# An attention block on one core: one addition of the early chains moved from VectorE to an accumulating transfer

## The chip, the cores and the metric

The kernel runs on one NeuronCore of a Trainium2 chip. The core has five engines that run side by side, each with its own instruction queue, worked off in order: TensorE (PE) multiplies matrices, VectorE (DVE) and ScalarE (ACT) work element by element, GpSimd (POOL) does simple passes over SBUF and can issue transfers, and SyncE (SP) issues most transfers. Sixteen DMA engines carry out the transfers. The metric is the time on the device in microseconds (us), lower is better.

## The reference

```
qkv = (x @ wqkv).reshape(B, S, 3, H, Dh).transpose(2, 0, 3, 1, 4)
q, k, v = qkv[0], qkv[1], qkv[2]
scores = einsum("bhqd,bhkd->bhqk", q, k) * Dh ** -0.5
p = softmax(scores, axis=-1)
o = einsum("bhqk,bhkd->bhqd", p, v)
out = o.transpose(0, 2, 1, 3).reshape(B, S, D) @ wo
```

B = 1, S = 2048 positions, D = 448 columns, H = 16 heads of Dh = 28; everything is bf16.

## The kernel before

**Sets and steps.** The 16 heads form four groups of four, each head padded to 32 rows, so that a group fills 128 partitions. The 2048 queries form four blocks of 512. A group and a block of queries make a *set*; there are 16, worked off in the order of `ORDER`. A *step* is one head of a set against one block of 128 keys: scores of 128 keys by 512 queries. A set has 4 x 16 = 64 steps. Scores of up to four heads run in TensorE at once, in different row groups; the products of the probabilities with the values (tile `o`, line 987) likewise, a *wave* of four heads in four column groups. A row of ones in the values gives the softmax denominator; there is no pass for the maximum, a bound worked out from the norms of queries and keys goes into the scores as additional rows of `QP`.

**Two ways to exponentiate.** ScalarE takes two steps in one instruction (`do_exp`, line 891: tile `a`, two banks wide, gives `pt`; there are ten `pt` tiles). VectorE takes one step (`do_a`, line 906) from a bank `d0`, `d1` or `m`: it adds a constant to the scaled score, clips at zero and writes int16, whose bits read as bf16 are a straight-line approximation of the exponential. One such line is coarse. So three lines are summed: four steps of a set form a *chain* with one int16 tile `I4` of 128 x 2048; the second and third line are `I4` plus 43 and plus 85 (`SHIFT`, added on VectorE in `do_add`, line 929, tiles `J1` and `J2`), and TensorE multiplies each of the three tiles with its own scaled copy of the values (`VT[k]`). So a step on VectorE costs one line, half an addition of four steps' width, and three value matmuls, where a step on ScalarE has one value matmul.

**The order.** Python code plays the five engines forward with assumed durations when the kernel is built, and emits each instruction when its engine is free: `pick_pe`, `pick_dve`, `pick_pool` and so on. The order of each engine's queue is fixed by this; on the chip, semaphores keep the dependencies. `d_more` opens a chain when fewer than `NCH` = 3 chains are in use and gives VectorE steps whenever a score bank is free; the remaining steps go to ScalarE. `pending` lists the tiles that wait for their value matmuls, each with the time at which it is expected, and `pv_cands` offers those whose time has come. `port` holds the times to which VectorE's additions and GpSimd's passes occupy what the code takes as a shared port: `can_add` in `pick_dve` lets no addition start in the planned time of a GpSimd pass, and `best` the other way round.

**GpSimd's passes** are, in the main part, the squares of keys and queries (line 297, for the norms) and the multiplication of a finished set by its reciprocals (line 1038). The reciprocals take this way (`finish_set`): VectorE copies the output bank `o` to `o_sb` (line 1016), SP gathers the denominators into `den`, VectorE inverts them, SP writes them to DRAM (`scr`) and spreads them over the partitions into `rr` (line 1035, 256 KB), GpSimd multiplies. The bank `o` is there once, so the next set's value matmuls wait for the copy.

**Other work on TensorE** is fitted in through bank `m`: the projections to keys, queries and values of coming groups (gated by the count of steps), norms, and the output projection. Where TensorE would idle for long, multiplications by zero (`dense`) are put in.

## Time and profile before

| what | value |
|---|---|
| median of 3 runs | 369.49 us (368.03 to 369.72) |
| the profiled execution | 368.69 us, span 366.9 us |
| granted TensorE clock | 1.000 |
| VectorE lines `I` | 292, 680 ns each |
| VectorE additions `J` | 146, all 128 x 2048, 724 ns each |
| ScalarE exponentials | 366, 1145 ns each, overlapping |
| GpSimd squares | 27 after the start, 1041 ns median |
| GpSimd multiplications | 15, 1263 to 1787 ns |
| transfers | 12.30 MB, mean 34 GB/s |

The span is the time from the first to the last instruction of one profiled execution. In the groups of instructions a line gives the source line, the engine, the operation, the tile written and the tiles read, the shape and the count; then busy time and mean duration; then the idle time before them and what ended it. Durations of successive instructions overlap on an engine, so an instruction's duration is longer than its share of the engine's time.

### The profile page before, as it was taken

What the parts mean: (1) busy time and instruction counts of PE and PEld (TensorE: products, weight loads), DVE (VectorE), ACT (ScalarE), POOL (GpSimd) and SP (SyncE); (2) the same over time, 40 slices, a digit from 0 to 9 for tenths busy, and PEclk for the clock granted to TensorE, in tenths of its full rate; (3) what the DMA queues carried; (4) which work ended last, traced back from release to release, by engine and by line L of the source; (5) the groups of instructions that cost most, each with busy time, mean ns of one, the idle gap of its engine ahead of it and who ended that gap; (6) DMA issues with size and microseconds to landing.
All of it is one profiled execution on the core that took longest, in us unless ns stands there. A gap on an engine that the chain in (4) does not pass through costs nothing.

```text
span 366.9 us, 10993 instructions
## 1 busy us (share of the span) xinstructions
PE 345.5 (94%) x4528; PEld 112.3 (31%) x4529; DVE 347.6 (95%) x646; ACT 348.9 (95%) x381; POOL 70.8 (19%) x103
## 2 busy tenths in 40 slices
PE   8999999999999999999889999989988999999985
PEld 4433233422233333232222222222222222222223
DVE  7799999999899999899999999999999999999983
ACT  4689999999999999999999999999999999999992
POOL 8952122123010413121010413201010101010010
PEclk9999999999999999999999999999999999999999
DMA  8510100011000000010000001100000001010101
GB/s 256 123 42 15 28 29 7 4 35 36 18 31 28 6 6 30 15 42 28 15 19 3 30 3 55 31 21 12 19 14 9 26 29 54 19 65 27 46 14 50
DMA packets 15050, 12.30 MB, mean 34 GB/s; under 512 B 6808, under 2 KB 13080, under 8 KB 15000
## 3 DMA queue, kind: packets, MB, share of 16 engines
q1 hardware_dynamic: 13448, 10.18, 9.7%
q10 hardware_dynamic: 1040, 1.02, 0.9%
q8 instruction: 35, 0.57, 0.7%
q0 software_dynamic: 512, 0.40, 0.5%
q14 instruction: 15, 0.12, 0.1%
HBM read 7.58 MB, written 1.96 MB: 26 GB/s over the span
## 4 chain that ended last, share of the span: by engine, by line
PE 34%; ACT 30%; DVE 27%; issue 7%; DMA 1%; DVEq 0%; ACTq 0%
ACT pt L891 30%; DVE I L906 12%; PE a L699 12%; PE o L987 9%; DVE J L929 7%; PE m L289 4%; PE m L282 4%; DVE QP L180 1%; DVE V L540 1%; DVE QA L436 1%; DVE KA L315 1%; DVE z L495 1%; PE d L699 1%; DVE o_sb L1016 1%; DVE V L552 1%
## 5 line engine op out<-in xcount | busy, mean ns | idle before, releaser
L891 ACT ACTIVATE pt<-a 128x1024 bf16<-128x1024 f32 x366 | 337.6, 1145 | 3.0 <-PE a L699 1.4
L906 DVE TENSOR_SCALAR I<-d 128x512 int16<-128x512 f32 x263 | 170.7, 680 | 3.8 <-PE d L699 3.4
L699 PE MATMUL a<-QP,KA 32*128 32x512 bf16 (+1 forms) x720 | 141.0, 381 | 12.2 <-ACT pt L891 11.2
L987 PE MATMUL o<-pt,V 128*32 128x512 bf16 x732 | 104.2, 384 | 0.0
L929 DVE TENSOR_SCALAR J<-I 128x2048 int16<-128x2048 int16 x146 | 101.8, 724 | 0.3
L699 PEld LDWEIGHTS <-KA 32*128 32x128 bf16 (+1 forms) x1041 | 48.7, 91 | 151.2 <-issue 148.3
L699 PE MATMUL d<-QP,KA 32*128 32x512 bf16 (+1 forms) x258 | 83.3, 383 | 1.3 <-DVE I L906 1.3
L987 PE MATMUL o<-J,V 128*32 128x512 bf16 x584 | 76.6, 384 | 0.4 <-DVE J L929 0.3
L987 PE MATMUL o<-I,V 128*32 128x512 bf16 x292 | 68.6, 384 | 0.7 <-DVE o_sb L1016 0.5
L987 PEld LDWEIGHTS <-V 128*32 128x32 bf16 x1608 | 28.6, 94 | 49.6 <-issue 47.0
L1038 POOL TENSOR_TENSOR xs<-o_sb,rr 128x512 bf16<-128x512 f32 x12 | 16.4, 1370 | 105.9 <-DMA rr<-scr 65.0
L282 PE MATMUL m<-XT,WRAW 112*32 112x512 bf16 x384 | 29.6, 384 | 0.2 <-DVE V L540 0.2
L297 POOL TENSOR_TENSOR sq<-KA 128x512 bf16<-128x512 bf16 x12 | 12.5, 1041 | 69.6 <-DVE KA L315 69.6
L297 POOL TENSOR_TENSOR sq<-QA 128x512 bf16<-128x512 bf16 x15 | 16.4, 1091 | 47.4 <-DVE QA L436 47.4
L906 DVE TENSOR_SCALAR I<-m 128x512 int16<-128x512 f32 x29 | 19.7, 680 | 0.4 <-PE m L699 0.4
L289 PE MATMUL m<-WRAW,XT 112*32 112x112 bf16 (+1 forms) x768 | 18.1, 230 | 0.2 <-DVE V L540 0.2
L1038 POOL TENSOR_TENSOR OTL<-o_sb,rr 128x512 bf16<-128x512 f32 x3 | 4.2, 1403 | 56.0 <-DMA rr<-scr 36.7
L289 PEld LDWEIGHTS <-XT 112*32 112x32 bf16 x768 | 11.7, 96 | 10.3 <-issue 10.1
L289 PE MATMUL m<-WO,xs 128*32 128x448 bf16 x156 | 12.5, 359 | 0.0
L436 DVE CAST QA<-m 128x512 bf16<-128x512 f32 x15 | 10.2, 683 | 1.1 <-PE m L282 0.5
L699 PE MATMUL m<-QP,KA 32*128 32x512 bf16 x29 | 11.1, 384 | 0.0
L289 PE MATMUL m<-sq,maskK 128*32 128x512 bf16 x108 | 10.8, 388 | 0.1
(113 smaller groups left out, 192.0 us busy)
## 6 DMA issues: line engine op xcount, KB each, us to landing
rr<-scr SPq DMA_DIRECT2D x15, 256.0 KB
QP<-QA SPq DMA_DIRECT2D x60, 28.0 KB
out_dram<-osb SPq DMA_DIRECT2D x12, 112.0 KB
WRAW<-in_wqkv_dram SPq DMA_DIRECT2D x3, 392.0 KB
xs<-in_x_dram ACTq DMA_DIRECT2D x4, 224.0 KB
xs<-in_x_dram SPq DMA_DIRECT2D x4, 224.0 KB
QP<-su SPq DMA_DIRECT2D x32, 2.0 KB
out_dram<-pt SPq DMA_DIRECT2D x2, 224.0 KB
```

Of the source, the lines that this page charges most:

```text
L180: nc.vector.memset(QP[c][k][z][:], 0.0)
L282: nc.tensor.matmul(out=ps[HP * i:HP * (i + 1), :], lhsT=w[:, cc, h * Dh:h * Dh + HP], rhs=XT[c][cc // 2][:, cc % 2, :], start=(cc == 0), s ...
L289: nc.tensor.matmul(out=out[r, :], lhsT=lhsT[:, r], rhs=rhs, start=start, stop=stop, tile_position=(0, HP * i), **k)
L297: nc.gpsimd.tensor_tensor(out=t[:], in0=src, in1=src, op=ALU.mult)
L315: nc.vector.tensor_scalar(out=KAt[(g, sc)][:], in0=src, scalar1=kmask[:, 0:1], scalar2=ones[:, 0:1], op0=ALU.mult, op1=ALU.add)
L436: nc.vector.tensor_copy(out=t[:], in_=held[key][:, 0:QW])
L699: nc.tensor.matmul(out=out_ap, lhsT=KAt[(g, j // XB)][r, (j % XB) * P:(j % XB + 1) * P], rhs=q[r, :], start=(n == 0), stop=(n == len(terms ...
L891: nc.scalar.activation(out=pt[:], in_=ps[:], func=ACT.Exp, scale=LN2 / 128.0)
L906: nc.vector.tensor_scalar(out=dst, in0=pd[:], scalar1=BIAS, scalar2=0.0, op0=ALU.add, op1=ALU.max)
L929: nc.vector.tensor_scalar(out=r[:, w], in0=ch["I"][:, w], scalar1=float(SHIFT[k]), scalar2=None, op0=ALU.add)
L987: nc.tensor.matmul(out=o[HP * i:HP * (i + 1), :], lhsT=VT[e["k"]][g, j // XB][:, j % XB, HP * i:HP * (i + 1)], rhs=e["ap"], start=(SETMM[k ...
L1038: nc.gpsimd.tensor_tensor(out=otile(g, c), in0=st["o_sb"][:], in1=st["rr"][:], op=ALU.mult)
```

## The change

A chain that is opened when its set has at least `FAR` = 24 steps left (the one just taken not counted) is called *far*. For a far chain GpSimd fills the `J1` tile with the constant 43 in every int16 (a memset of 1024 words of 32 bits), and when the four lines are in `I4`, GpSimd issues a transfer that adds `I4` onto `J1` in place. The code expects it to have landed 6.0 us after an issue that takes 0.65 us, and plans the value matmuls of `J1` for then. VectorE makes only the addition for `J2`. For other chains VectorE makes both, as before.

Every GpSimd pass gets a wait for the VectorE operation last emitted among those that use the shared port (`after_shared`; `cur["shared"]` is set by the additions, the scaled values, the norms' small operations and the reciprocals). The transfer's issue does not get it.

Buffers: `I4` and `J1` four instead of three, `J2` three; a chain is opened by new conditions (`dve_ok`) that look at the chain four before. To make room, `osb` has two tiles instead of four, `o_sb` and `rr` one instead of two, and the first query tile shares its buffer with `z`. The copy to `o_sb` needs the multiplication of the set before (`("OT",) + set_gc(s - 1)`). Assumed durations: GpSimd's square 1.08 instead of 1.15, the multiplication 1.3 instead of 1.4, the spread's landing 7.0 instead of 5.5, and the inversion is planned 2.0 later.

```diff
+    NCH = 4
+    NCH2 = 3
+    NJ = 4
+    FAR = 24
+    ACC_LAND = 6.0
...
+        if op.after is not None:
+            op.after(end)
...
+    def after_shared(m):
+        if "shared" in cur:
+            tc.add_manual_dep(m.ins, cur["shared"].ins.name,
+                              mybir.DependencyInfo(mybir.DependencyClass.Sync, mybir.DependencyReason.DATA),
+                              reason="GpSimd's pass stays behind VectorE's")
...
-        nc.gpsimd.tensor_tensor(out=t[:], in0=src, in1=src, op=ALU.mult)
+        after_shared(nc.gpsimd.tensor_tensor(out=t[:], in0=src, in1=src, op=ALU.mult))
...
     def dve_ok(t, k):
-        if chain["cur"] is None and chain["used"] >= NCH:
-            return False
+        if chain["cur"] is None and len(chain["all"]) >= NCH:
+            old = chain["all"][-NCH]
+            if not j1_free() or not used_up(old, 0) or any(a[0] is old for a in adds) or old["acc"] is None or old["acc"] > t:
+                return False
...
+                chain["all"].append(ch)
+                ch[1] = wk.tile([P, HG * QW], I16, name="J1", bufs=NJ)
+                if sum(len(q) for q in remain[step[0]]) >= FAR:
+                    ch["far"] = True
+                    far_chain(ch)
...
+    def close(ch, m):
+        ch["m"] = m
+        adds.append([ch, m, 2 if ch["far"] else 1])
+        if ch["far"]:
+            accumulate(ch, m)
+
+    def used_up(ch, k):
+        return ch["m"] is not None and ch["got"][k] == ch["m"]
+
+    def j1_free():
+        return len(chain["all"]) < NJ or used_up(chain["all"][-NJ], 1)
+
+    def add_ok(a):
+        if a[2] == 1:
+            return True
+        n = chain["all"].index(a[0])
+        return n < NCH2 or used_up(chain["all"][n - NCH2], 2)
+
+    def far_chain(ch):
+        n = len(chain["all"])
+        fill = SHIFT[1] * 65537
+
+        def emit():
+            m = nc.gpsimd.memset(ch[1][:].bitcast(I32), fill)
+            after_shared(m)
+
+        ch["id"] = n
+        add("POOL", 1.08, emit, gives=[("fill", n)], pri=20, port=True)
+
+    def accumulate(ch, m):
+        w = slice(0, m * QW)
+        ch["acc"] = None
+
+        def emit():
+            nc.gpsimd.dma_start(out=ch[1][:, w], in_=ch["I"][:, w], accum_op=ALU.add)
+
+        def landed(end):
+            at = ch["acc"] = end + ACC_LAND
+            for n in range(m):
+                pending.append({"step": ch["steps"][n], "k": 1, "ap": ch[1][:, n * QW:(n + 1) * QW].bitcast(BF16),
+                                "ready": at, "pt": None, "ch": ch})
+
+        evt[("I4", ch["id"])] = (free["DVE"], "DVE")
+        add("POOL", 0.65, emit, need=[("fill", ch["id"]), ("I4", ch["id"])], gives=[("acc", ch["id"])], pri=10, port=True)
+        ops["POOL"][-1].after = landed
...
-        nc.vector.tensor_scalar(out=r[:, w], in0=ch["I"][:, w], scalar1=float(SHIFT[k]), scalar2=None, op0=ALU.add)
+        cur["shared"] = nc.vector.tensor_scalar(out=r[:, w], in0=ch["I"][:, w], scalar1=float(SHIFT[k]), scalar2=None, op0=ALU.add)
...
-            st["o_sb"] = wk.tile([P, QW], F32, name="o_sb")
+            st["o_sb"] = wk.tile([P, QW], F32, name="o_sb", bufs=1)
...
-        add("DVE", 0.61, evac, need=[("Oset", s)], gives=[("osb", s)], rel="o", pri=-5)
+        add("DVE", 0.61, evac, need=[("Oset", s)] + ([("OT",) + set_gc(s - 1)] if s else []), gives=[("osb", s)], rel="o", pri=-5)
...
-        add("DVE", 0.16, recip, need=[("den", s)], gives=[("rec", s)], pri=50, port=True)
+        add("DVE", 0.16, recip, need=[("den", s)], gives=[("rec", s)], pri=50, lag=2.0, port=True)
...
-        add("SP", 0.5, spread, need=[("scr", s)], gives=[("rr", s)], land=5.5, pri=2)
-        add("POOL", 1.4, mul, need=[("rr", s)], gives=[("OT", g, c)], pri=60, port=True)
+        add("SP", 0.5, spread, need=[("scr", s)], gives=[("rr", s)], land=7.0, pri=2)
+        add("POOL", 1.3, mul, need=[("rr", s)], gives=[("OT", g, c)], pri=60, port=True)
...
-        can_add = adds and port["POOL"] <= t
+        can_add = adds and port["POOL"] <= t and add_ok(adds[0])
```

More of the change, by code (lines that the diff above doesn't have):

```diff
@@ L33, in __init__ @@
         self.need, self.gives, self.pri = list(need), list(gives), pri
+        self.after = None
         self.acq, self.rel, self.gate, self.lag, self.land, self.cols, self.port = acq, rel, gate, lag, land, cols, port
@@ L73 @@
     NPT = 10
-    NCH = 3
+    NCH = 4
[3 more added lines that the diff above has]
+    ACC_LAND = 6.0
     DRAIN = 8
@@ L322, in k_job @@
         add("DVE", 0.72, evac, need=[key + (split - 1,)], gives=[key], rel=bank, pri=pri)
-        add("POOL", 1.15, lambda: square(key, KAt[(g, sc)][:]), need=[key], gives=[("ksq", g, sc)], pri=pri, port=True)
+        add("POOL", 1.08, lambda: square(key, KAt[(g, sc)][:]), need=[key], gives=[("ksq", g, sc)], pri=pri, port=True)
     def kn_job(g, bank, pri, gate=0):
@@ L342, in spread_rows @@
             kmt[g] = wk.tile([P, 1], F32, name="kmt")
-            nc.vector.reduce_max(out=kmt[g][:], in_=b[:], axis=AX.X)
+            cur["shared"] = nc.vector.reduce_max(out=kmt[g][:], in_=b[:], axis=AX.X)
         for sc in range(NQC):
@@ L428, in evac @@
             if first:
-                t = qtt[0] = wk.tile([P, QW], BF16, name="qt0", bufs=1)
+                t = qtt[0] = wk.tile([P, QW], BF16, name="z", bufs=1)
             else:
@@ L452, in q_job @@
         else:
-            add("POOL", 1.15, lambda: square(key, QAt[(g, c)][:]), need=[key], gives=[("qsq", g, c)], pri=pri, port=True)
+            add("POOL", 1.08, lambda: square(key, QAt[(g, c)][:]), need=[key], gives=[("qsq", g, c)], pri=pri, port=True)
             add("SP", 2.4, rows, need=[key, ("QZ", c, g % 2)] + ([("Oset", ORDER.index((g - 2, c)))] if g > 1 else []),
@@ L497, in bound @@
             held[("su",) + key] = su = wk.tile([P, QW], BF16, name="su", bufs=1)
-            nc.vector.tensor_scalar(out=su[:].bitcast(I16), in0=z[:].bitcast(I16), scalar1=0.5, scalar2=HALFE,
+            cur["shared"] = nc.vector.tensor_scalar(out=su[:].bitcast(I16), in0=z[:].bitcast(I16), scalar1=0.5, scalar2=HALFE,
                                     op0=ALU.mult, op1=ALU.add)
@@ L551, in scale @@
             flat = (lambda v: v.rearrange("p t g e -> p (t g e)")) if g is None else (lambda v: v.rearrange("p t e -> p (t e)"))
-            nc.vector.tensor_scalar(out=flat(VT[k][g, b]), in0=flat(VT[0][g, b]), scalar1=WT[k], scalar2=None, op0=ALU.mult)
+            cur["shared"] = nc.vector.tensor_scalar(out=flat(VT[k][g, b]), in0=flat(VT[0][g, b]), scalar1=WT[k], scalar2=None, op0=ALU.mult)
         gs = [g] if g is not None else list(range(GH, G))
@@ L568, in evac @@
         def evac():
-            held[key + ("sb",)] = osb = wk.tile([P, D], BF16, name="osb", bufs=4)
+            held[key + ("sb",)] = osb = wk.tile([P, D], BF16, name="osb", bufs=2)
             nc.vector.tensor_copy(out=osb[:], in_=held.pop(key)[:, 0:D])
@@ L669 @@
     pts_used = [0]
-    chain = {"cur": None, "used": 0}
+    chain = {"cur": None, "all": []}
     a_fifo = []
@@ L788, in d_more @@
             if ch is None:
-                chain["used"] += 1
                 ch = chain["cur"] = {"I": wk.tile([P, HG * QW], I16, name="I4", bufs=NCH), "s": step[0], "n": 0,
-                                     "open": 0, "next": 0, "done": 0}
+                                     "got": [0] * NTERM, "m": None, "next": 0, "done": 0, "acc": 0.0, "far": False}
+                chain["all"].append(ch)
[3 more added lines that the diff above has]
+                    far_chain(ch)
             taken.append(ch["next"])
@@ L909, in do_a @@
         ch.setdefault("steps", []).append(step)
-        ch["open"] += NTERM
         ch["done"] += 1
@@ L913, in do_a @@
         if ch["done"] == HG:
-            adds.append([ch, HG, 1])
+            close(ch, HG)
         else:
@@ L922, in flush @@
             chain["cur"] = None
-            adds.append([ch, ch["n"], 1])
+            close(ch, ch["n"])
     def do_add(t):
@@ L927, in do_add @@
         w = slice(0, m * QW)
-        r = ch[k] = wk.tile([P, HG * QW], I16, name=f"J{k}", bufs=NCH)
-        nc.vector.tensor_scalar(out=r[:, w], in0=ch["I"][:, w], scalar1=float(SHIFT[k]), scalar2=None, op0=ALU.add)
+        if k == 2:
+            ch[k] = wk.tile([P, HG * QW], I16, name="J2", bufs=NCH2)
+        r = ch[k]
+        cur["shared"] = nc.vector.tensor_scalar(out=r[:, w], in0=ch["I"][:, w], scalar1=float(SHIFT[k]), scalar2=None, op0=ALU.add)
         end = port["DVE"] = t + m * QW * 0.00026 + 0.068
@@ L996, in do_pv @@
                 else:
-                    e["ch"]["open"] -= 1
-                    if e["ch"]["open"] == 0 and e["ch"] is not chain["cur"] and e["ch"]["done"] == e["ch"]["n"]:
-                        chain["used"] -= 1
+                    e["ch"]["got"][e["k"]] += 1
         if not any(remain[s]) and outst[s] == 0:
@@ L1024, in recip @@
             st["rec"] = wk.tile([P, HG * QW // P], F32, name="rec")
-            nc.vector.reciprocal(out=st["rec"][:], in_=st["den"][:])
+            cur["shared"] = nc.vector.reciprocal(out=st["rec"][:], in_=st["den"][:])
         def scatter():
@@ L1033, in spread @@
             scr = st["scr"]
-            st["rr"] = wk.tile([P, QW], F32, name="rr")
+            st["rr"] = wk.tile([P, QW], F32, name="rr", bufs=1)
             nc.sync.dma_start(out=st["rr"][:], in_=scr[:].unsqueeze(1).to_broadcast([HG, HP, QW]))
         def mul():
-            nc.gpsimd.tensor_tensor(out=otile(g, c), in0=st["o_sb"][:], in1=st["rr"][:], op=ALU.mult)
-        add("DVE", 0.61, evac, need=[("Oset", s)], gives=[("osb", s)], rel="o", pri=-5)
+            m = nc.gpsimd.tensor_tensor(out=otile(g, c), in0=st["o_sb"][:], in1=st["rr"][:], op=ALU.mult)
+            after_shared(m)
+        add("DVE", 0.61, evac, need=[("Oset", s)] + ([("OT",) + set_gc(s - 1)] if s else []), gives=[("osb", s)], rel="o", pri=-5)
         add("SP", 0.6, gather, need=[("osb", s)], gives=[("den", s)], land=1.5, pri=2)
-        add("DVE", 0.16, recip, need=[("den", s)], gives=[("rec", s)], pri=50, port=True)
+        add("DVE", 0.16, recip, need=[("den", s)], gives=[("rec", s)], pri=50, lag=2.0, port=True)
         add("SP", 0.35, scatter, need=[("rec", s)], gives=[("scr", s)], land=1.1, pri=2)
-        add("SP", 0.5, spread, need=[("scr", s)], gives=[("rr", s)], land=5.5, pri=2)
-        add("POOL", 1.4, mul, need=[("rr", s)], gives=[("OT", g, c)], pri=60, port=True)
+        add("SP", 0.5, spread, need=[("scr", s)], gives=[("rr", s)], land=7.0, pri=2)
+        add("POOL", 1.3, mul, need=[("rr", s)], gives=[("OT", g, c)], pri=60, port=True)
     def best(eng, t):
@@ L1240 @@
                              start=(gg == 0), stop=(gg == G - 1))
-        osb = wk.tile([P, D], BF16, name="osb", bufs=4)
+        osb = wk.tile([P, D], BF16, name="osb", bufs=2)
         if tq % 2 == 0:
```

## The prediction

> **What bounds the kernel now.** I read the table of engines first, then the busy time by stage, the groups, the waits, the timelines of single engines, and the transfers last. Span and engines, on the page of the profiled run:

> ```profile
> span 366.9 us, 10993 instructions
> PE 345.5 (94%) x4528; PEld 112.3 (31%) x4529; DVE 347.6 (95%) x646; ACT 348.9 (95%) x381; POOL 70.8 (19%) x103
> ```

> Three engines are full, so nothing gets faster by relieving one alone: the scheduler must hand work from one to another. Busy time in three stretches (first row to 170 us, second to 235, third to 357):

> ```profile
> 44.00:170.00 126.00, 123.07 (x1767) 40.74 (x1764) 121.36 (x216) 124.97 (x137) 24.92 (x22) 1.00 0.08 23
> 170.00:235.00 65.00, 61.94 (x711) 18.13 (x711) 63.87 (x108) 64.90 (x72) 12.09 (x11) 1.00 0.07 21
> 235.00:357.00 122.00, 112.53 (x1290) 33.27 (x1286) 120.19 (x202) 121.13 (x132) 8.49 (x6) 1.00 0.09 27
> ```

> The columns are length, then busy TensorE, weight loads, VectorE, ScalarE, GpSimd. VectorE and ScalarE are full throughout; TensorE idles 6.0 us in the first 191 us (3%) and 9.5 us in the last 122 (8%). The groups that the change trades:

> ```profile
> L891 ACT ACTIVATE pt<-a 128x1024 bf16<-128x1024 f32 x366 | 337.6, 1145 | 3.0 <-PE a L699 1.4
> L906 DVE TENSOR_SCALAR I<-d 128x512 int16<-128x512 f32 x263 | 170.7, 680 | 3.8 <-PE d L699 3.4
> L929 DVE TENSOR_SCALAR J<-I 128x2048 int16<-128x2048 int16 x146 | 101.8, 724 | 0.3
> L929 DVE TENSOR_SCALAR J<-I x146: 627/684/1766, 23.8 to 355.5; 128x2048 int16<-128x2048 int16 x146
> ```

> The 146 additions are two lines of 73 chains. In VectorE's timeline one addition or one line I follows the next every 0.60 us; ScalarE's exponentials, two steps each, follow one another every 0.904 us. One of the longest additions, 1.76 us against a median of 0.68, belongs to this pair (GpSimd, then VectorE):

> ```profile
> 205.13 1.27 POOL L1038 TENSOR_TENSOR xs<-o_sb,rr 128x512 bf16<-128x512 f32 x1
> 205.19 1.76 DVE L929 TENSOR_SCALAR J<-I 128x2048 int16<-128x2048 int16 x1
> ```

> An addition that starts 0.06 us after a GpSimd pass ends about one pass later: the two do not run together. The transfers that come nearest to the new one: the weight loads issued by GpSimd (issue time, then time to landing), and GB/s in 40 slices of 0.175 us around one spread of the reciprocals (256 KB, issued at 101.37):

> ```profile
> L205 POOL DMA_DIRECT2D WO<-in_wo_dram x16: 507/507/705, 13.9 to 21.9; - x16
> DMA to landing us min/median/max: 1.8/2.0/3.3
> ```

> ```profile
> GB/s 36 11 0 0 0 0 0 0 0 0 0 0 0 0 0 35 35 117 94 94 94 105 129 94 94 82 94 117 82 105 82 47 0 47 0 0 0 0 0 0
> ```

> That spread moves at about 100 GB/s; the page's first slice, the loads, shows 256 GB/s.

> **The change, part by part.**

> *Removed.* A chain opened with at least 24 steps of its set left loses its first addition. Counting score matmuls in the trace, a set being 64 steps, 51 of the 73 chains open so (six of them right at 24). That is 51 x 0.60 = 30.6 us of VectorE, and that only.

> *What it buys.* A step moved from ScalarE to VectorE saves 0.904 / 2 = 0.452 us there and costs 0.60 for its line plus its share of additions (two for four lines, less the 51/73 = 0.70 that goes), (2 - 0.7) x 0.60 / 4 = 0.195, so 0.795 here. Balanced, v us freed on VectorE shorten both by 0.452 v / (0.452 + 0.795) = 0.36 v: 11 us for 30.6.

> *Fills.* 51 memsets of 1024 words; the nearest row, 1024 elements cleared by GpSimd, has 1.02 us. GpSimd goes from 71 to 71 + 51 x (1.02 + 0.65) = 156 us (0.65 is the issue time that the scheduler now assumes; the weight loads show 0.51), far from full, but each fill and each issue is a time in which an addition blocks, or the issue does. So far the additions lose 146 x (724 - 684) ns = 5.8 us to 42 passes, 0.14 each. At that rate 102 new passes cost 14 us; with the new wait they could cost nothing and the 5.8 could come back. Range -5.8 to +14, I take +4: the wait fixes one side only, and the scheduler keeps additions out of the planned time of a pass.

> *The wait.* [...] Behind a waiting pass stand, in order, squares (TensorE's norm matmuls need them), fills, issues and the multiplication by the reciprocals. Passes that got stretched (1.4 to 1.8 us against 1.04 and 1.27) number some 7 of 42. A pass is held at most one addition, 0.68 us; the consumers come microseconds later. Zero, or 51 x 0.68 us on the landing below if that cover is gone.

> *Fewer fillers.* Additions are what VectorE does while no score bank is ready. It waits 4.1 us for scores now; I take 4 us more (0 to 8). With the blocking, 30.6 - 4 - 4 = 22.6 us are freed: 8.1 us of span.

> *TensorE.* An exponential fewer is a score group fewer: 0.32 us and 0.13 of turn in its timeline (score groups start 0.32 before the next wave, a wave of four takes 0.23, the turn is the rest). Two steps on VectorE bring four value matmuls more, one wave, 0.23. Net -0.22 us where ScalarE gets 0.904 shorter. Up to 235 us (191 of 313 us, 61% of the main part) there is next to no idle time, so between a quarter (0.22 / 0.904) and all of that part's gain arrives: 8.1 x (0.39 + 0.61 x 0.25) = 4.4 to 8.1 us. I take 6.3.

> *The transfer.* 512 KB read, 512 KB of destination read, 512 KB written; no row shows an accumulating transfer. Below: 2.0 us (weight loads, small) + 512 KB at 256 GB/s = 4.1 us from issue to landing. Above: 2.0 + 1 MB at 100 GB/s = 12.5. Nearest I hold 1 MB at 256 GB/s, 6.1 us: long rows on all 16 engines, like the loads, and twice the reads. The scheduler expects 0.65 + 6.0 = 6.65 us, and places the value matmuls there, so 6.1 costs nothing. [...]

> *Set borders.* A set takes about 20.5 us, 0.32 a step. A chain opened at 24 left closes some 5.7 us later and lands at 12.3, while the last score falls at 7.7 and its set otherwise ends 2 us after: 2.6 us late. From 32 left on nothing is late. Some 9 of 16 sets have such a chain, 1.3 us each on average: up to 12 us of later release of the output bank, covered by ten exponential tiles (9 us) except where TensorE has no slack to catch up. I take 1.3.

> *The rest.* One buffer for o_sb and rr makes a set's evacuation wait for the multiplication of the set before: o_sb at 318.2, multiplication done at 330.1, next o_sb at 339.7, so 9 us of slack. SP's queue gets no new issue, but its gathers, spreads and QP rows share the 16 engines with 51 transfers of 2 to 10 us: zero while the added delay stays below 9 us. Two osb buffers for twelve stores, the shared z tile (first used at 32.1, qt0 last read at 23.9), and the scheduler's new durations: 0, at most 1 us either way by another order.

> Sum against the profiled run's own 368.69 us (span 366.9 and 1.8 around it; the median of the runs is 369.49, 0.8 above): -6.3 + 1.3 = -5.0, 363.7; against the median, 364.5. I say **364**.

> **The rivals.**

> *Late landing (slower).* The value matmuls stand in TensorE's order at the planned landing; if it comes d later, TensorE, with 15.5 us of idle time in 313, 0.30 a transfer, stops for the rest: 51 x (d - 0.3). It eats the gain at d = 0.4, a landing 7.05 us after issue; at 7.2 us it gives 364 + 13 = 377, at 7.65 some 400. For it: the slow spread. Against it: the loads' rate.

> *Locked passes.* VectorE blocks on all 102 passes at the old rate: 30.6 - 14 - 4 = 12.6 us freed, 4.5 us of span, of which TensorE and the borders leave about 1: 368. [...] If each issue lost one addition's 0.60 us, 6.1 us would become 6.7, the edge of the late landing.

> *TensorE takes it all, or the limit of 24 and the four J1 tiles let fewer chains through (no change).* Half as many chains with TensorE's lower share: (15.3 - 4) x 0.36 = 4.1 us, of which 4.4/8.1 or 2.2 us arrive, less 1.3: 368.

> *The single o_sb tile (slower).* If spread and multiplication come 9 us later behind transfers and fills, VectorE's copy stops, and with it the output bank; 1 us beyond that in 15 sets gives 379. Against it: one landing at a time, about every 7 us.

> **How the numbers follow.** 0.5% (1.8 us) is about what this kernel's runs can tell from no change. Forecast 0.50 (its own range 359 to 367); locked passes and fewer chains together 0.15, mostly within 0.5%; late landing 0.25; o_sb 0.10. The range runs from 358 (30.6 us freed whole, 11 us) to 377 (landing at 7.2). Faster 0.52, same 0.12, slower 0.36.

> **What would show it.** Additions down from 146 to about 95 and still 0.68 us; lines I up from 292 by some 18, exponentials down by 9; fills of about 1.0 us; landings under 6.65 us, and no large wait of TensorE's value matmuls on a transfer into J1; o_sb copies not waiting on GpSimd. It is wrong if the J1 waits sum to more than about 15 us, if additions stretch, or if ScalarE idles behind TensorE in the first 235 us.

## The result: slower, and the profile after

The changed kernel takes **387.51 us** (median of 4 runs, 385.83 to 387.63) against 369.38 before on the same chip: a ratio of 1.0488, with a 95% interval of 1.0459 to 1.0517. I had said 364, with 358 to 377 as the range. The sign was wrong, and the time lies 10.5 us above the range. Some kernels below had a slower state in one or two of their runs: the ratios leave these runs out, the medians do not.

From the page of the changed kernel's profiled execution, the lines that answer to those shown of before (engines, clock in 40 slices, the queue of GpSimd's transfers, the main groups):

```profile
span 385.9 us, 11165 instructions
PE 347.7 (90%) x4503; PEld 111.1 (29%) x4503; DVE 334.2 (87%) x611; ACT 341.9 (89%) x371; POOL 189.0 (49%) x233
...
PEclk9999999699988999999999999999999999896999
...
q0 software_dynamic: 9872, 34.49, 47.4%
...
L911 ACT ACTIVATE pt<-a 128x1024 bf16<-128x1024 f32 x356 | 330.5, 1097 | 27.7 <-PE d L713 20.8
L926 DVE TENSOR_SCALAR I<-d 128x512 int16<-128x512 f32 x284 | 186.1, 682 | 21.9 <-PE d L713 21.1
...
L961 POOL MEMSET J<- 128x1024 int32 x65 | 68.0, 1052 | 58.8 <-DVE J L996 15.6
...
L996 DVE TENSOR_SCALAR J<-I 128x2048 int16<-128x2048 int16 x91 | 70.0, 788 | 0.8 <-PE o L1054 0.6
...
J<-I POOLq DMA_DIRECT2D x65, 512.0 KB, 5.0
```

The last line's 5.0 is the median time in us from issue to landing; in the line of the queue stand its packets, the MB moved, and the time that the packets took as a share of the 16 engines' span.

The reader is to see three things.

- **The exchange took place.** Ten exponentials fewer (356 for 366), 20 lines `I` more (312 with the 28 of bank `m`, for 292), 55 additions fewer (91 for 146), 65 fills and 65 transfers.
- **No engine is the bound any more.** VectorE went from 95% to 87%, ScalarE from 95% to 89%, and TensorE from 94% to 90%. ScalarE now idles 27.7 us before its exponentials, where it was 3.0.
- **TensorE's clock is not always 10 tenths.** Before, it was 1.00 up to the end. Now it falls to half for 6.8 us at 70.5, 3.4 at 104.7, 3.4 at 118.3, 3.4 at 330.0 and 6.8 at 347.0: 23.8 us.

The waits of the changed kernel (engine, line, what was waited for; us in total, times, longest):

```profile
DVE I L926 <- PE d L713: 21.1, 39, 3.2
ACT pt L911 <- PE d L713: 20.8, 16, 5.6
...
POOL xs L1103 <- DMA rr<-scr: 11.1, 5, 4.3
...
DVE osb L584 <- DMA out_dram<-osb: 5.3, 1, 5.3
PE m L296 <- DVE osb L584: 5.2, 2, 5.0
...
PE o L1054 <- DMA J<-I: 4.4, 9, 1.1
...
PE a L713 <- DMA QP<-su: 3.5, 2, 3.3
...
DVE rec L1090 <- DMA den<-o_sb: 3.0, 2, 2.6
```

TensorE waits for the new transfers for 4.4 us only. That is not all that they cost: the chain of work that ended last, followed back from the end of the kernel, passes through their flights for 12% of the span, and through SP's transfers (`rr`, `scr`, `out_dram`, `den`, `QP`) for 10%:

```profile
DMA J<-I 12%; ACT pt L911 11%; PE a L713 11%; DVE I L926 11%; PE o L1054 9%; PE m L296 5%; DVE J L996 5%; PE m L289 3%; DMA rr<-scr 3%; DMA scr<-rec 3%; DMA out_dram<-osb 2%; DVE o_sb L1081 1%; PE o L627 1%; DMA den<-o_sb 1%; DMA QP<-su 1%
```

The other DMA waits are for SP's old, small transfers: the spread of the reciprocals, the stores of the output, the bound's rows, the gather of the denominators. From issue to last packet, as medians before and after, they went: gather 1.52 to 3.71 us, write of the reciprocals 1.04 to 2.52, spread 4.33 to 5.51 (longest 8.33), store 1.58 to 3.57 (longest 7.86).

How one becomes late shows in its packets. A `J1` transfer was issued at 46.13 us and a gather at 46.6. Packets started, in steps of 0.5 us:

```
from us                47.1  47.6  48.1  48.6  49.1  49.6  50.1
J1's, 4096 bytes          2    30    23    25    24    24     0
the gather's, 64 bytes    0     0     0     0     0     4   124
```

The gather stands behind most of the transfer: its first packet starts at 49.87 us, when 112 of the transfer's 128 rows have started (8 rows of 346 ns for each of 16 engines), and it lands 3.93 us after its issue. Gathers that meet no transfer still land after 1.5 to 1.6 us; those that meet one take 3.7 to 4.8, and nothing lies between.

One place shows what a late transfer does. The changed kernel's timeline, GpSimd and then VectorE (start, duration, idle time before):

```profile
64.32 1.26 POOL L1103 TENSOR_TENSOR xs<-o_sb,rr 128x512 bf16<-128x512 f32 x1 [4.08 <-DMA rr<-scr]
65.54 0.85 POOL L972 DMA_DIRECT2D J<-I  x1
66.12 1.24 POOL L961 MEMSET J<- 128x1024 int32 x1
67.04 1.32 POOL L311 TENSOR_TENSOR sq<-KA 128x512 bf16<-128x512 bf16 x1
68.03 1.16 POOL L972 DMA_DIRECT2D J<-I  x1
68.61 1.55 POOL L961 MEMSET J<- 128x1024 int32 x1
...
67.50 3.20 DVE L996 TENSOR_SCALAR J<-I 128x2048 int16<-128x2048 int16 x1
```

The spread landed 7.7 us after its issue (4.4 before). GpSimd stood 4.08 us at the multiplication, with two issues, two fills and a square queued behind it. Then all of them ran back to back, and the addition that VectorE's order put there took 3.20 us instead of 0.68. TensorE waited 2.3 us for its result, and then this (stretches of the changed kernel; the columns are those shown of before, the granted clock is the third number from the end):

```profile
44.00:70.50 26.50, 24.08 (x427) 8.71 (x420) 24.98 (x41) 25.77 (x29) 15.17 (x16) 1.00 0.62 120
70.50:77.30 6.80, 6.54 (x51) 1.26 (x50) 5.02 (x11) 3.35 (x4) 2.12 (x2) 0.50 0.61 117
```

For 6.8 us TensorE is busy at half speed and ScalarE starts 4 exponentials where, at 0.904 us each, it starts seven otherwise.

### The profile page after: what moved, and what is told of

Read it like the earlier page. It is cut to its first block, busy times and chain, and to the rows that moved or that the text cites. A ratio compares the mean times of both kernels' runs of the same rounds, so it can differ in the third digit from the quotient of the medians.

```text
span 385.9 us, 11165 instructions
## 1 busy us (share of the span) xinstructions
PE 347.7 (90%) x4503; PEld 111.1 (29%) x4503; DVE 334.2 (87%) x611; ACT 341.9 (89%) x371; POOL 189.0 (49%) x233
## 3 DMA queue, kind: packets, MB, share of 16 engines
q0 software_dynamic: 9872, 34.49, 47.4%
q10 hardware_dynamic: 1040, 1.02, 0.9%
## 4 chain that ended last, share of the span: by engine, by line
PE 33%; DMA 24%; DVE 20%; ACT 11%; issue 7%; SPq 2%; POOL 1%; DVEq 0%; POOLq 0%; ACTq 0%
DMA J<-I 12%; ACT pt L911 11%; PE a L713 11%; DVE I L926 11%; PE o L1054 9%; PE m L296 5%; DVE J L996 5%; PE m L289 3%; DMA rr<-scr 3%; DMA scr<-rec 3%; DMA out_dram<-osb 2%; DVE o_sb L1081 1%; PE o L627 1%; DMA den<-o_sb 1%; DMA QP<-su 1%
## 5 line engine op out<-in xcount | busy, mean ns | idle before, releaser
L911 ACT ACTIVATE pt<-a 128x1024 bf16<-128x1024 f32 x356 | 330.5, 1097 | 27.7 <-PE d L713 20.8
L926 DVE TENSOR_SCALAR I<-d 128x512 int16<-128x512 f32 x284 | 186.1, 682 | 21.9 <-PE d L713 21.1
L972 POOL DMA_DIRECT2D J<-I x65 | 59.6, 923 | 88.4 <-DVE I L926 75.5
L713 PE MATMUL d<-QP,KA 32*128 32x512 bf16 (+1 forms) x279 | 97.8, 393 | 0.4 <-DVE I L926 0.2
L961 POOL MEMSET J<- 128x1024 int32 x65 | 68.0, 1052 | 58.8 <-DVE J L996 15.6
L713 PEld LDWEIGHTS <-KA 32*128 32x128 bf16 (+1 forms) x1041 | 44.4, 92 | 153.4 <-issue 146.8
L1054 PE MATMUL o<-I,V 128*32 128x512 bf16 x312 | 75.9, 398 | 1.9 <-DVE o_sb L1081 1.8
L996 DVE TENSOR_SCALAR J<-I 128x2048 int16<-128x2048 int16 x91 | 70.0, 788 | 0.8 <-PE o L1054 0.6
L1054 PEld LDWEIGHTS <-V 128*32 128x32 bf16 x1648 | 31.9, 95 | 61.5 <-issue 54.3
L289 PE MATMUL m<-XT,WRAW 112*32 112x512 bf16 x384 | 30.6, 394 | 0.3 <-DVE QA L450 0.2
L296 PE MATMUL m<-WRAW,XT 112*32 112x112 bf16 (+1 forms) x768 | 18.5, 235 | 0.0
L296 PEld LDWEIGHTS <-XT 112*32 112x32 bf16 x768 | 12.3, 98 | 8.4 <-issue 8.1
L584 DVE CAST osb<-m 128x448 bf16<-128x448 f32 x12 | 7.4, 617 | 5.9 <-DMA out_dram<-osb 5.3
```

Source lines behind the costliest of these rows:

```text
L289: nc.tensor.matmul(out=ps[HP * i:HP * (i + 1), :], lhsT=w[:, cc, h * Dh:h * Dh + HP], rhs=XT[c][cc // 2][:, cc % 2, :], start=(cc == 0), s ...
L296: nc.tensor.matmul(out=out[r, :], lhsT=lhsT[:, r], rhs=rhs, start=start, stop=stop, tile_position=(0, HP * i), **k)
L584: nc.vector.tensor_copy(out=osb[:], in_=held.pop(key)[:, 0:D])
L713: nc.tensor.matmul(out=out_ap, lhsT=KAt[(g, j // XB)][r, (j % XB) * P:(j % XB + 1) * P], rhs=q[r, :], start=(n == 0), stop=(n == len(terms ...
L911: nc.scalar.activation(out=pt[:], in_=ps[:], func=ACT.Exp, scale=LN2 / 128.0)
L926: nc.vector.tensor_scalar(out=dst, in0=pd[:], scalar1=BIAS, scalar2=0.0, op0=ALU.add, op1=ALU.max)
```

## The experiments

Each ratio is against the kernel before, run beside it on the same chip. The chips differ: on them the kernel before took 368.5 to 369.4 us (medians), so a difference between the times of two experiments is good to about 1 us. Where an edit makes the planner find a new order (`FAR` = 1000 and 44, the later landing, SP's landings, the spread held back), a difference to the changed kernel has that order in it too.

### The same queues without the load

```diff
-            nc.gpsimd.dma_start(out=ch[1][:, w], in_=ch["I"][:, w], accum_op=ALU.add)
+            nc.gpsimd.dma_start(out=ch[1][:, 0:32], in_=ch["I"][:, 0:32], accum_op=ALU.add)
```

> The changed kernel with the accumulating transfer cut to 32 of its 2048 columns (64 bytes a row); the rest of J1 keeps the fill, so the output leaves out most of the second line. The order of every engine's instructions is that of the changed kernel. Theory (traffic: the 34 MB of the new transfers slow SP's gathers, spreads, query rows and stores on the same 16 DMA engines; a few consumers stand still for 2 to 6 us, and TensorE's clock halves after each): SP's spread lands after 4.3 us again instead of 5.5, the waits on the store, on QP and on den vanish, the granted clock is 1.00, and the time falls from 387.5 to 358-366. Rival (shared port: fills and issues block VectorE's additions, 788 ns mean): these stay, so the time stays above 380. Rival (late landing of J1): 4.4 us of such waits at most, 383.

Measured: 365.72 us, 0.9922 (0.9884 to 0.9959), in the range that I had named; but the clock still falls to half for 10.2 us, which I had not expected (a later section finds a stall behind it). From the page of this kernel:

```profile
span 363.4 us, 11131 instructions
PE 341.3 (94%) x4502; PEld 113.3 (31%) x4503; DVE 325.0 (89%) x611; ACT 339.0 (93%) x371; POOL 187.3 (52%) x233
...
PEclk9999999999996999999999999999999989999999
...
q0 software_dynamic: 9872, 0.94, 4.7%
...
L996 DVE TENSOR_SCALAR J<-I 128x2048 int16<-128x2048 int16 x91 | 61.1, 690 | 1.0 <-PE o L1054 0.7
```

All five queues hold the same instructions in the same order as in the changed kernel; fills, issues and waits are there too. So the bytes cost 387.51 - 365.72 = **21.8 us**, by the load that they put on the engines and by the later landing of `J1` together (median 2.2 us here, 5.0 there). Fills and issues do not hurt the additions by themselves: 690 ns each with every GpSimd pass in its place, 788 with the full transfer. In the changed kernel 21 additions overlap an issue and no pass, and these have 685 ns.

Because the order is the same, each exponential of one profile has its partner in the other. How late the k-th one of the changed kernel starts:

```
exponential           0    10    50    60    80    90   100   220   230   310   320   330   350
thin, start us     18.9  28.9  65.4  74.7  92.9 102.3 118.4 228.2 237.5 312.0 321.2 330.4 348.7
changed, start us  18.9  30.2  66.9  80.8  99.5 111.8 127.1 239.2 249.9 324.8 336.2 351.5 370.6
later by, us        0.0   1.3   1.5   6.2   6.7   9.5   8.7  11.0  12.4  12.7  15.0  21.1  21.9
```

The loss sits in a few jumps. 4.6 us (k 50 to 60) is the late spread shown above. 2.1 (80 to 100) begins with VectorE's reciprocal waiting 2.6 us for the gather; behind it stands the copy of a query tile, and TensorE waits 1.9 us for that. 6.1 (320 to 330) is VectorE waiting 5.34 us for a store that landed after 7.86 us. These three places, all with a late SP transfer at their head, make 12.8 of 21.9. At two others, 1.4 (220 to 230) and 2.3 (310 to 320), TensorE waits for `J1` (1.6 and 1.0 us), beside a wait of VectorE's output copy for GpSimd. The first 1.3 us (0 to 10) arise at about 25 us, before the first transfer into `J1` is issued at 29.5, so they are not its cost.

### Without far chains

```diff
-    FAR = 24
+    FAR = 1000
```

> The changed kernel with the limit of 24 raised to 1000, so that no chain is far: no fill, no transfer, VectorE makes all additions, but the buffers, the waits of GpSimd's passes and the assumed durations are the new ones. Traffic theory: 366-371, no change against the kernel before. Rival (the cut buffers and the new waits cost by themselves): 375 or more.

Measured: **364.44 us**, 0.9875 (0.9846 to 0.9904), the fastest version that computes everything, and faster than I had expected. What is left of the change are its waits, buffers and durations. The tile `J`, additions with shortest, median and longest in ns, in this kernel:

```profile
L996 DVE TENSOR_SCALAR J<-I x148: 624/682/694, 23.8 to 352.6; 128x2048 int16<-128x2048 int16 x148
```

Not one addition is stretched; before, the longest took 1766 ns and eight took over 800.

### The waits alone

The kernel without far chains, with the waits taken off GpSimd's passes; all queues in the same order.

```diff
-        if "shared" in cur:
+        if False:
```

> e4 without the waits of GpSimd's passes; the order is that of e4. If the waits make e4 faster than the kernel before (they keep GpSimd's passes off VectorE's additions, which have 681 ns in e4 against 724 before), the additions go back to about 725 and the time to 367-370. If the fourth chain buffer or the new order does, 364-365 stays.

Measured: 367.30 us (366.82 to 368.11), 0.9958 (0.994 to 0.9976). Its additions:

```profile
L996 DVE TENSOR_SCALAR J<-I x148: 622/681/1768, 24.5 to 356.1; 128x2048 int16<-128x2048 int16 x148
```

The stretched additions are back. The waits are worth 367.30 - 364.44 = 2.9 us, and the time is in the range named for them; what else differs from before (a fourth chain, other durations) gives the remaining 0.4%.

### Idle plain copies beside it

The kernel without far chains, with a plain 512 KB copy to DRAM, which nobody reads, for each of the 62 chains of 74 that open with at least 24 steps left (`far2`):

```diff
...
+        if ch["far2"]:
+            to = dram.tile([P, HG * QW], I16, name="idle", bufs=4)
+            nc.gpsimd.dma_start(out=to[:, 0:m * QW], in_=ch["I"][:, 0:m * QW])
```

> e4 (no far chain, 364.4 us) and, for each of the 47 chains that would be far, a transfer of its closed 512 KB to a scratch in DRAM that nobody reads, issued by GpSimd without a fill and without a place in the schedule; the order of the other engines is that of e4. Traffic theory: SP's spreads, gathers and rows slow down (gather 1.5 -> 3 us or more), the stalls and the half clock come back, 372-385. Rival (what costs is the landing of J1, which nobody waits for here): 364-367.

Measured: 368.44 us, 0.9987 (0.997 to 1.0005), 4.0 above its partner. From its page:

```profile
PEclk9999999999999999999999999999999999999999
...
q0 software_dynamic: 9440, 32.91, 22.8%
```

The same bytes, half the load: 163 ns for a row of 4 KB against 346 for an accumulated one. The gather's median is 1.59 us, the store's 2.83. The 4.0 us come in six jumps of 0.3 to 0.9, and the clock never falls. The time lies between the two ranges that I had named, and even the 4.0 us are hardly the load's: behind one jump VectorE's output copy waits 1.0 us for GpSimd, and four come 2 to 6 us after an addition of 1137, 1849, 1990 or 1902 ns, stretched beside a pass; ahead of three of these passes GpSimd had just made one of the new issues. So 512 KB a chain is not dear as such. What makes the accumulating transfer dear, the doubled time of a row or that its landing is waited for, this run does not tell.

### Half the width

```diff
-            nc.gpsimd.dma_start(out=ch[1][:, w], in_=ch["I"][:, w], accum_op=ALU.add)
+            nc.gpsimd.dma_start(out=ch[1][:, 0:1024], in_=ch["I"][:, 0:1024], accum_op=ALU.add)
```

> The changed kernel with the accumulating transfer cut to 1024 of 2048 columns (the second half of J1 keeps the fill; the output leaves that out); the order of all engines is that of the changed kernel (387.5 us) and of e1 (32 columns, 365.7). J1 lands about 1.4 us earlier, some 3.5 us after the issue against 6.65 planned, so it is hardly ever late; the extra load of the DMA engines is half. If the load's delay of SP's transfers is what costs, 372-382; if late landings of J1 cost, 364-369.

Measured: 368.95 us (365.92 to 372.06), 1.0000 (0.9962 to 1.0038). The same order again, so three widths stand side by side:

| columns | a row, ns | share of 16 engines | gather that meets one, us | half clock, us | time, us |
|---|---|---|---|---|---|
| 32 | 29 | 4.7% | 1.6 to 1.7 | 10.2 | 365.72 |
| 1024 | 187 | 27.4% | 2.1 to 2.9 | 13.6 | 368.95 |
| 2048 | 346 | 47.4% | 3.7 to 4.8 | 23.8 | 387.51 |

The first half costs 3.2 us, the second 18.6. The time is in the range that I had named for late landings of `J1` (364 to 369), not in that for the load (372 to 382), and TensorE waits for no `J1` here. But the width changes both: `J1` lands after 3.5 us instead of 5.0 (medians), and a wider row makes a meeting longer (8 x 187 = 1.5 us, 8 x 346 = 2.8) and more frequent. That the order has slack for the small delays would give the same time without any late `J1`; the run does not separate the two. The 3.4 us of half clock that the half width has more than the thin one, at 332.7, follow a wait of VectorE's for a store, 2.1 us.

### Four output tiles

`osb` takes the squares' four buffers, so that VectorE need not wait for a store. The order is unchanged.

```diff
-            held[key + ("sb",)] = osb = wk.tile([P, D], BF16, name="osb", bufs=2)
+            held[key + ("sb",)] = osb = wk.tile([P, QW], BF16, name="osb", tag="sq", bufs=4)[:, 0:D]
...
```

> The changed kernel with four output tiles again (they take the buffers of the squares, which are dead by then); the order of all instructions is the same. Traffic theory: the one wait of 5.3 us on a store and the half clock for 6.8 us after it go, 387.5 -> 377-381. Rival (buffers are the cause, not traffic): the same wait goes and the loss with it, and the two other large stalls go too, below 373.

Measured: 391.44 us (385.5 to 394.18), 1.0496 (1.0419 to 1.0574). By the ratio this is the time of the changed kernel again (1.0488): no gain, against both expectations. The wait for the store is gone, and this stands in its place (waits of this kernel):

```profile
PE o L1054 <- DMA J<-I: 10.8, 8, 3.8
...
PE o L1054 <- DVE J L996: 2.5, 2, 2.3
```

The `J1` waits went from 4.4 to 10.8 us; the largest, at 351 us and at 85 us, lie where the changed kernel has none. Against the thin transfer its profile loses 0.4 us where the store had cost 6.1, and 6.0 just behind it. Half clock: 30.6 us. When each transfer moves, others meet; here TensorE stands for late `J1` tiles where VectorE stood for a store.

### A later planned landing

```diff
-    ACC_LAND = 6.0
+    ACC_LAND = 9.0
```

> The changed kernel with the landing of J1 planned 9.0 us after the issue instead of 6.0, so that the value matmuls of J1 stand later in TensorE's order; the traffic is the same. Late-landing rival: the waits on J1 go and with them what follows, 372 or less. Traffic theory: SP's transfers are as slow as before and their consumers as early, 380-392.

Measured: 377.00 us (374.47 to 377.6), 1.0209 (1.0167 to 1.025), between the two ranges. TensorE no longer waits for `J1` and the clock is half for 6.8 us only. What stays are late SP transfers: GpSimd waits for the spread, VectorE 4.3 us for a store and 2.0 for the gather, TensorE 2.1 for the bound's rows. With the same traffic, a plan that lets `J1` come later takes 10.5 us less, so late `J1` tiles may hold a good part of the loss; but the order differs, so the gain can't be put down to the landing alone.

### An order that knows SP's landings

Rows of the queries and of the bound planned to land after 3.5 and 5.0 us instead of 1.6 and 1.4, gather 4.0 with the inversion right behind it, write 2.9, spread 8.0; the bound's rows first in SP's queue; four output tiles.

```diff
-            gives=[("QA", g, c) for c in cs], land=1.4, pri=1)
+            gives=[("QA", g, c) for c in cs], land=5.0, pri=0)
...
-        add("SP", 0.6, gather, need=[("osb", s)], gives=[("den", s)], land=1.5, pri=2)
+        add("SP", 0.6, gather, need=[("osb", s)], gives=[("den", s)], land=4.0, pri=2)
...
```

> The changed kernel with the schedule told of the slower SP transfers: gather 4.0 instead of 1.5 with the inversion right after it, scatter 2.9 instead of 1.1, spread 8.0 instead of 7.0, rows of queries 3.5 instead of 1.6, rows of the bound 5.0 instead of 1.4 and ahead of the other issues; four output tiles as in e3. Traffic theory, by way of in-order consumers: the long waits go, the clock stays at 1.00, 362-372. Rival (the engines themselves slow the work, by shared port or landing): no better than 380.

Measured: 399.55 us (397.49 to 405.86), 1.0815 (1.0774 to 1.0855): the opposite of what I expected, and within what the rival allowed. Up to 178 us it runs level with the thin transfer or up to 5 us ahead of it; then the order itself waits at the set borders (ScalarE idles 3 to 5 us at 193, 272, 297 and 320), and the clock is half for 23.8 us ahead of the tail. Told of the delays, this planner seems to move the wait into the order; that is a reading of the trace, and no run tests it.

### One stall that is not the load's

The thin transfer keeps a stall at 103 us: SP's queue holds the spread of the third set (256 KB) ahead of eight small rows of the next group's bound, and the first row lands 3.5 us after its issue instead of 1.2. Here the spread waits until those rows are issued, first with the thin transfer, then with the full one.

```diff
-        add("SP", 0.5, spread, need=[("scr", s)], gives=[("rr", s)], land=7.0, pri=2)
+        add("SP", 0.5, spread, need=[("scr", s)] + ([("QA", 1, 0)] if s == 2 else []), gives=[("rr", s)], land=7.0, pri=2)
```

> e1 (transfer of 32 columns; the output leaves most of the second line out), and the spread of the third set's reciprocals is issued behind the rows of the second group's bound, not ahead of them. In e1 and in the changed kernel these rows wait behind 256 KB on SP's queue and hold TensorE for 3 us at about 105 us. Expected: that stall and the half clock after it go, 356-362 against 365.7. Rival (other stalls take its place): 364 or more.

> The changed kernel with the same edit as e10, the full transfer; the order of all engines is that of e10. Traffic theory: what the transfers cost shows again as the difference from e10, 15-25 us, so 374-384; TensorE's clock is halved for 10 us or more, after waits on J1, on the spread's followers and on SP's rows. Rival (the 22 us between the changed kernel and e1 hang on that one stall): 365 or less.

Measured: thin 361.34 us (360.66 to 363.47), 0.9813 (0.9779 to 0.9847); full 376.78 us (374.09 to 379.74), 1.0198 (1.0156 to 1.0239). The wait that disappears, from the thin transfer as it was,

```profile
PE a L713 <- DMA QP<-su: 3.0, 1, 3.0
```

and the clock of the thin one with the spread held back:

```profile
PEclk9999999999999999999999999999999999999999
```

So the edit takes 4.4 us off the thin transfer's time and 10.7 off the changed kernel's. It also moved instructions in the queues of VectorE and GpSimd, so not all of that need be this one stall. The bytes cost 376.78 - 361.34 = 15.4 us in this order as well, where both kernels have the same queues. And 361.34 shows what 65 additions off VectorE are worth with next to no load and no stall: 3.1 us against the version without far chains, across two orders.

### Fewer far chains

```diff
-    FAR = 24
+    FAR = 44
```

> The changed kernel with the limit raised from 24 to 44 steps: about half as many transfers, and none that lands near its set's end. Traffic theory: 368-378, between e4 (none, 364.4) and the changed kernel. If single late landings near the border of the sets cost, 364 or less.

Measured: 368.15 us (367.13 to 370.45), 0.9986 (0.9966 to 1.0006). 39 transfers, 30.2% of the engines, 115 additions of 719 ns; half clock for 3.4 us. GpSimd still waits 13.3 us for spreads. The time is in the range named for the load. It equals that of the kernel before only because the new waits and order are in it too: beside the version without far chains (364.44) these 39 chains lose 3.7 us, more than their additions give.

### The load without a late J1

Half the transfer to `J1`, the rest (896 columns) to a scratch tile that nobody reads, and four output tiles:

```diff
...
-            nc.gpsimd.dma_start(out=ch[1][:, w], in_=ch["I"][:, w], accum_op=ALU.add)
+            nc.gpsimd.dma_start(out=ch[1][:, 0:1024], in_=ch["I"][:, 0:1024], accum_op=ALU.add)
+            nc.gpsimd.dma_start(out=idle[:], in_=ch["I"][:, 1024:1920], accum_op=ALU.add)
```

> e9 with the load brought back: J1 waits for 1024 columns only (the rest keeps the fill, the output leaves that out), and right behind this transfer a second one adds 896 columns onto a scratch in SBUF that nobody reads (four output tiles as in e3, for the room). The order of the other engines is that of the changed kernel; the load of the DMA engines is 94% of its, the landing of J1 near that of e9. If the delay of SP's transfers under the full load is what costs, 380-390; if the lateness of J1 is, 367-372 as e9 (369.0); between, the two share the 18.5 us that lie between e9 and the changed kernel in that proportion.

Measured: 400.58 us (396.17 to 407.79), 1.0837 (1.0794 to 1.0881). It lies outside every range that I had named, and does not decide what it was made for. 65 more issues of about 1 us went into GpSimd's queue, and it waited 9.3 us for earlier idle transfers. From its waits:

```profile
PE m L299 <- POOL sq L314: 7.5, 5, 2.6
...
PE o L1058 <- DMA J<-I: 5.3, 3, 3.6
PE o L1058 <- DVE o_sb L1085: 5.1, 4, 2.3
```

TensorE waits 7.5 us for GpSimd's squares, which nothing else delayed this much (0.8 in the changed kernel). It shows GpSimd's queue as an amplifier: what held its head here held all that was behind.

What stays open: how the 15 to 22 us divide between late SP transfers and late `J1` tiles. The pairing of the exponentials puts more than half on the places where an SP transfer is late; the half width, the later planned landing and the four output tiles speak for a large part of `J1`; no run isolates either. A run of the thin transfer without most of the fills was planned and gave no result, so the price of the fills by themselves is open too.

## Why the prediction was wrong

**Right: the exchange.** Forecast 9 exponentials fewer and 18 lines more; measured 10 and 20. I expected 51 far chains of 73 from counting the old trace, and there were 65 of 78; the order without far chains opens 62 of 74 so, which says that my count was low. Fills 1.05 us on average (951 ns median) for 1.02.

**Right in the median, open in the tail: the landing.** 5.0 us median against 6.1, planned 6.65. The late-landing rival, priced as 51 times a common delay, did not happen that way: 4.4 us of TensorE's waits, not 13. But of the 49 landings that the profile times (4.5 to 9.2 us from issue), 7 came later than planned, and what this tail costs stays open, as said above. That the destination is read as well was my assumption: the trace counts 512 KB a transfer, and shows no more of it than the time of a row, 346 ns for 4 KB.

**The step that failed: "SP's queue gets no new issue, but its gathers, spreads and QP rows share the 16 engines ...: zero while the added delay stays below 9 us".** The delays were 1 to 6 us, as that sentence allowed, and yet three places that begin with one of them hold 12.8 of the 21.9 us that the profile of the changed kernel loses to the thin one. The 9 us were the slack of the last consumer, the next set's output copy, and that one waits only 2.5 us. But each operand stands first in front of an engine that works in order: the spread holds GpSimd's multiplication and everything behind it, the gather holds VectorE's reciprocal, the store a buffer. "Two osb buffers ...: 0" failed in the same way, at 5.3 us. I compared the delay with the slack of the data and not with that of the queue. How much of the rest of the loss is late `J1` tiles stays open.

**The term that was missing: the clock.** Before, it was 1.00 throughout and I had no term for it. In five places 1.2 to 3.3 us of TensorE's idle time were followed by 3.4 or 6.8 us at half speed. Of the late spread's 4.6 us, 2.3 come with the stall and the rest with the half clock.

**Locked passes.** Half right. The shared port is the code's assumption: no run shows a port, only additions stretched beside a pass (1.76 us for 0.68 at 205 us). With the passes in their planned places the additions take 690 ns, less than before; the waits gain 2.9 us where I said zero. With the passes piled up behind a late operand, 91 x (788 - 684) = 9.5 us are lost, inside my range of up to 14, by a cause I did not have. What I had asked of the issues has an answer too: the 21 that overlap an addition take 1021 ns on average, the other 44 876, and the additions beside them lose nothing (685 ns).

**What the gain would have been.** I forecast 6.3 us for the freed time. With next to no load and without the stall in SP's order, 65 additions gave 3.1 us over the version that keeps them on VectorE: VectorE is then busy 90% of the time, and the freed time was largely not used. That the thin transfer's 365.7 lies near my 364 is luck: the new waits and order gave 4.2 us (368.65 to 364.44) that I had put at nothing, the additions gave half of what I had forecast, and the stall in SP's order took 4.4.

**The signs named beforehand.** Stretched additions and ScalarE idling behind TensorE in the first 235 us both came; the sum of the `J1` waits, which I had put first, stayed under its limit of 15 us.

## What to carry to other kernels

Before work is moved to the DMA engines, ask which small transfers share them and which in-order queue stands at each: the slack that counts is that of the next instruction behind the waiting one, not of the data's last use. A transfer can delay what it meets by most of its share on an engine (the gather by 2 to 3 us here, behind 8 rows of 346 ns), and half of one can cost far less than half (3.2 of 21.8 us here): compare its share (rows per engine times time per row) with the tightest planned landing. In a kernel whose TensorE runs full, price each new stall of over 1 us with a spell of half clock behind it (3.4 or 6.8 us here); and where passes of two engines stretch each other, as GpSimd's and VectorE's do here (1.77 us for 0.68), a wait that keeps the one behind the other may be worth having by itself (2.9 us here).

## What the hardware showed that I had not expected

**The accumulated rows took twice the time of the copied ones**: 346 ns (SBUF to SBUF, the changed kernel) against 163 (SBUF to DRAM, the idle copies) for 4 KB on one engine; accumulated, 187 for 2 KB (half the width) and 29 for 64 bytes (the thin transfer).

**An addition was stretched across several passes in a row.** 3.20 us, where the longest before was 1.77; the four output tiles, the full transfer with the spread held back and the split transfer have one each of 3.17 to 3.20 too. In the case shown, it runs from 67.50 to 70.70 us, beside the end of the square (68.36) and the whole fill behind it (68.61 to 70.16), with an issue between them and no gap.
